# Retention followed by a soft mixture of experts on one core: the transposes to natural layout move in front of the intra-chunk products, the group's logits and dispatch move to a step's end, the selection rounds move later, and the output blocks become 256, 128, 128 columns wide

## The chip, the cores and the metric

The kernel runs on one NeuronCore of a Trainium2 chip. The metric is the device time of one execution in microseconds (us): the median of several runs. One execution was also taken by the hardware profiler; its page and its trace are what is read below. TensorE has two rows in the profile, PE (matmuls) and PEld (weight loads, which overlap them). DVE is VectorE, ACT ScalarE, POOL GpSimd, and SP SyncE, whose queue issues every DMA of this kernel.

## The reference

Four sequences of 768 tokens and 8 heads of width 64 go through a retention (a decaying linear attention), and its output, seen as 3072 tokens of 512 channels, through a soft mixture of 8 experts with 4 slots each:

```
for t: state = gamma[h] * state + k[t] v[t]^T ;  y[t] = q[t] state / 8
x = y as (3072, 512)
logits = x @ phi                                   # 3072 x 32 slots
d = softmax of logits over the tokens  ; slot_in = d.T @ x
slot_out[e] = relu(slot_in[e] @ w1[e]) @ w2[e]     # 512 -> 1024 -> 512, 8 experts
c = softmax of logits over the slots   ; out = c @ slot_out
```

All data are 32-bit floats. The weights w1 and w2 are 33.6 MB of the 55.8 MB read; the output is 6.3 MB.

## The kernel before, in words

**Retention.** There are 24 steps (4 sequences of 6 chunks of 128 tokens). Step i works, on TensorE, in this order: `scores(i+1)` (L225: keys times queries of the next chunk into the two PSUM tiles sc0 and sc1; VectorE masks them, L229, into two tiles A; ScalarE copies the transposed keys, L233, where they are not loaded), `inter(i)` (L247: the state `sst` times the queries into the PSUM tiles y0 and y1), `intra(i)` (L258: v times A, added into y0 and y1), `state(i)` (L280, copied to `sst` by ScalarE, L282; left out in the last chunk of a sequence), and `natural(i-1)` (L288: four transposes of the previous chunk's result into the PSUM bank misc, copied by ScalarE into xn, L290). After `intra(i)`, VectorE's `scale(i)` (L267, two instructions each for y0 and y1) writes the chunk's result yT. There is one buffer of y0, y1, sc0, sc1 and misc each, so `inter(i+1)` waits until `scale(i)` has read y0 and y1. GpSimd multiplies each v by its decay (L207) after its DMA.

**Groups.** Four steps are a group g. In the first step of the next group (ph 0) the logits of the group's 512 tokens are made in misc (`logits_mm`, L300; maximum L320, nm L321, exponential on ScalarE L323, a transposed copy lb on VectorE L328), and at that step's end the exponentials are transposed (`dispatch_p`, L333, copied by ScalarE L335). In the second step (ph 1) `dispatch_u` (L342) multiplies them with the four xn, and VectorE adds that to acc (L353). `combine_weights` makes the softmax over the slots from lb: on VectorE cm (L359), the difference cb (L361), after ScalarE's exponential the sum and its inverse cz (L364 to L366), on GpSimd their product (L367), and on VectorE the transpose into cT (L368).

**Experts.** After step 23 come the last group's logits, `natural(23)`, whose copy to xn is one VectorE instruction, the last dispatch, and the slots' inputs siT. `hidden(g, k)` (L533) multiplies them with w1 for two halves g of the experts; `hidden_t` (L546) transposes the result. `split_c` cuts cT into a rounded part and a rest (VectorE, L384 and L385), and four `c_round(n)` (L395) spread it by a selection matrix into two PSUM buffers named sm, from which ScalarE casts it (L401) into the tiles c4T that the output products need.

**Output.** The 512 output channels are done in blocks. For each, 16 pieces of work fc (L623) multiply with w2; then `finish` copies the sum (L586), spreads it with one matmul (L590), splits it (L592, L593), multiplies it with c4T (L605, six products per 128 channels), copies these out of PSUM on VectorE and ScalarE (L611, L608) and sends 128 channels x 1024 tokens per DMA (L609). `finish` is a generator: its pieces run between the fc of the next block, in places set by the tables Y1, Y2 and BURST; the last block's run alone.

**Queues.** TensorE's order is that of the code. The other engines' orders, and that of the DMAs on SP, are set by the scheduler that builds the program. Weights stream ahead of use: 34 tiles of 512 KB during the retention, then into the key/query buffers (L163), into half tiles (L168) and into freed tiles (L171). kq, v and kn are the DMAs of a step: keys and queries (four buffers), values, and keys in natural layout for some steps.

Of the kernel before, what the change touches and what calls it, by code (L numbers as in the profile page):

```python
# [12 lines left out]
ALU = mybir.AluOpType  # L13
# [3 lines left out]
B, H, S, D = 4, 8, 768, 64  # L17
# [19 lines left out]
NPRE = 34  # L37
BLOCKS = [(0, 128), (128, 256), (384, 128)]
NRING = 34
# [6 lines left out]
FPS = {256: 4, 192: 4, 128: 8, 64: 8}  # L46
Y1 = (3, 4, 2)
Y2 = (4, 6, 2)
GRP = 4
# [42 lines left out]
def retention_soft_moe_kernel(  # L92
# [117 lines left out]
    def scores(i):  # L210
# [5 lines left out]
        for hf in range(2):  # L216
            scv = sct[hf][:, :, 0:384].rearrange("p r (g n) -> p r g n", n=192)
            for gg in range(2):
                g = 2 * hf + gg
                for late in range(2):  # L220
                    for r in range(2):
                        o = (late if g % 2 == 0 else 1 - late) * D
                        kb = KB[2 * g + late]
                        n = 2 + state - late
                        nc.tensor.matmul(scv[o:o + D, r, gg, late * D:(late + n) * D],  # L225
                                         s["kq"][r * D:(r + 1) * D, kb * D:(kb + 1) * D],
                                         blocks(s["kq"], r, NB - (2 - late) * QS[g], QS[g], n),
                                         start=True, stop=True)
            nc.vector.tensor_tensor(A[hf], scv[:, :, :, 0:C],  # L229
                                    mask.unsqueeze(1).broadcast_to([128, 2, 2, C]), ALU.mult)  # L230
            if state:
                kn = s["kn"].rearrange("p (g r) e -> p r g e", r=2)[:, :, 2 * hf:2 * hf + 2]
                nc.scalar.copy(kn, scv[:, :, :, C:C + D])  # L233
# [50 lines left out]
    def natural(i):  # L284
# [4 lines left out]
        s["xn"] = half_tile()  # L289
        (nc.vector.tensor_copy if i == NSTEP - 1 else nc.scalar.copy)(s["xn"], xp)  # L290

# [45 lines left out]
    def dispatch_u(g):  # L337
# [6 lines left out]
        if g == 0:  # L344
            nc.scalar.copy(acc, u)
        elif last:
# [4 lines left out]
        else:  # L351
            nc.vector.scalar_tensor_tensor(zrun, zrun, q["al"], q["z"], ALU.mult, ALU.add)
            nc.vector.scalar_tensor_tensor(acc, acc, q["al"], u, ALU.mult, ALU.add)  # L353

# [72 lines left out]
    scores(0)  # L427
    for e, hs_ in ((nc.gpsimd, slice(4, 8)), (nc.vector, slice(0, 4))):
        e.tensor_tensor(st[0]["v"][:, hs_], st[0]["v"][:, hs_],
                        vsc[:, 0, hs_].unsqueeze(2).broadcast_to([128, 4, D]), ALU.mult)  # L430
    budget = 0.0
    for i in range(NSTEP):
# [6 lines left out]

        def rest():  # L440
            intra(i)
            scale(i)
            state(i)

        if i == 0:
            inter(i)
            rest()
        if not last:
# [7 lines left out]
        if i + 3 < NSTEP:  # L456
            load_kq(i + 3)
        if g > 0 and ph == 0:
            logits_mm(g - 1, range(GRP))
            logits(g - 1)  # L460
        if g > 0 and ph == 1:
            dispatch_u(g - 1)
        if i > 0:
            rest()
        if g > 0 and ph == 1:
            combine_weights(g - 1)
        if i > 0:
            natural(i - 1)
        if g > 0 and ph == 0:
            dispatch_p(g - 1, i)  # L470
    psc_phase.__exit__(None, None, None)
# [96 lines left out]
    hidden_t(0)  # L568
    c_round(0)
    for k in (2, 3):  # L570
        load_weights(4)
        hidden(1, k)
        c_round(k - 1)
    load_weights(len(weights))
    c_round(3)

# [40 lines left out]
    for cb, (c0, w) in enumerate(BLOCKS):  # L617
        op = pe.tile([128, 512], F32, name=("sc0", "sc1")[cb % 2])
        for g in range(2):
            for fc in range(NFC):  # L620
# [6 lines left out]
                if cb == 0 and g == 0 and fc == 2:  # L627
                    hidden_t(1)
                for f in pend:
                    next(f, None)  # L630
# [65 lines left out]
```

## Time and profile before

| | |
|---|---|
| time, median of 3 runs | 176.27 us (175.4 to 176.44) |
| profiled execution | 174.94 us, span 173.0 us |
| TensorE busy | 149.7 us (86%) of the span |
| VectorE, ScalarE, GpSimd busy | 93.2, 48.1, 31.9 us |
| DMA moved | 62.51 MB, mean 361 GB/s |
| mean granted TensorE clock | 0.984 |

The span is the time from the first to the last recorded instruction; the execution's own time is 1.94 us more. The profile's views used here are the page's groups of instructions by line, the chain of work that ended last (each piece follows what released it), the timeline of one engine (with, in brackets, how long the engine had been idle and what ended that), and a table of stretches with each engine's busy time, the granted clock, the share of the DMA engines and what they moved.

### The profile page before, as it was taken

The numbers are of one execution on the slowest core, as the hardware profiler recorded it, in microseconds if no ns is written. First come the engines' busy times: TensorE is split into PE (matmuls) and PEld (weight loads), VectorE is DVE, ScalarE is ACT, GpSimd is POOL, SyncE is SP. The second block draws the span as 40 slices with busy tenths as digits, with TensorE's granted clock in tenths as the row PEclk, the third lists the DMA queues.
The fourth block names the chain that finished last, engine by engine and source line by source line (L and its number), as shares of the span: only waits on it lengthen the run. The fifth ranks groups of instructions, "written<-read, shape, count | busy, mean of one in ns | idle before, by whom it ended". The sixth has DMA issues, their size and how long they took to land.

```text
span 173.0 us, 6469 instructions
## 1 busy us (share of the span) xinstructions
PE 149.7 (86%) x2752; PEld 106.4 (62%) x2752; DVE 93.2 (54%) x278; ACT 48.1 (28%) x122; POOL 31.9 (18%) x46
## 2 busy tenths in 40 slices
PE   8589966999899999979999799999977898999700
PEld 2378955689669767868679668853322493566500
DVE  1566645777876787757775685434132131425720
ACT  2133322343513342324133422310102700303510
POOL 0243214213331322031421322400200000000000
PEclk9999999999999999999999999999999999999985
DMA  5999999999999999999999998999999999444993
GB/s 186 322 408 390 368 403 408 403 392 403 402 397 405 403 401 407 396 405 401 403 403 402 406 405 330 279 352 328 357 412 418 410 405 367 184 194 175 393 405 123
DMA packets 20765, 62.51 MB, mean 361 GB/s; under 512 B 2304, under 2 KB 2688, under 8 KB 20736
## 3 DMA queue, kind: packets, MB, share of 16 engines
q1 hardware_dynamic: 20736, 62.09, 92.9%
q8 instruction: 22, 0.36, 0.9%
q14 instruction: 7, 0.06, 0.1%
HBM read 55.79 MB, written 6.29 MB: 359 GB/s over the span
## 4 chain that ended last, share of the span: by engine, by line
PE 69%; DMA 13%; DVE 6%; issue 5%; SPq 1%; ACT 1%; DVEq 0%
PE y L258 11%; PE sc L225 10%; PE sc L623 9%; PE misc L288 7%; PE y L247 5%; DMA kq<-in_kq_dram 5%; DMA r<-in_w_dram 5%; PE y L533 4%; PE S L280 4%; DMA h<-in_v_dram 3%; PE misc L300 3%; PE misc L342 2%; PE misc L533 2%; PE S L533 2%; PE sm L605 2%
## 5 line engine op out<-in xcount | busy, mean ns | idle before, releaser
L229 DVE TENSOR_TENSOR h<-sc,kt 128x512 f32<-128x512 f32 x48 | 31.4, 686 | 18.6 <-PE sc L225 14.6
L207 POOL TENSOR_TENSOR h<-h,kt 128x512 f32<-128x512 f32 x23 | 24.1, 1049 | 61.8 <-DMA h<-in_v_dram 46.3
L267 DVE SCALAR_TENSOR_TENSOR h<-y,kt,ysc 128x128 f32<-128x128 f32 x96 | 27.3, 343 | 4.5 <-PE y L258 4.2
L258 PE MATMUL y<-h 128*64 128x128 f32 x384 | 26.9, 279 | 3.1 <-DVE h L229 2.1
L225 PE MATMUL sc<-kq 64*64 64x128 f32 (+2 forms) x768 | 26.2, 270 | 2.4 <-issue 0.9
L258 PEld LDWEIGHTS y<-h 128*64 128x64 f32 x384 | 20.8, 136 | 11.2 <-issue 6.8
L225 PEld LDWEIGHTS sc<-kq 64*64 64x64 f32 x768 | 21.3, 133 | 7.1 <-issue 4.0
L288 PE MATMUL misc<-kt,h 128*128 128x128 f32 x96 | 15.6, 285 | 2.4 <-DVE cb L361 1.3
L290 ACT COPY h<-misc 128x512 f32<-128x512 f32 x23 | 13.5, 586 | 14.4 <-PE misc L288 12.5
L282 ACT COPY sst<-S 128x256 f32<-128x256 f32 x20 | 7.4, 372 | 33.6 <-PE S L280 33.5
L280 PE MATMUL S<-h 128*64 128x64 f32 x320 | 13.0, 222 | 1.4 <-issue 1.4
L247 PE MATMUL y<-kq,sst 64*64 64x128 f32 x320 | 13.7, 273 | 0.2 <-issue 0.2
L280 PEld LDWEIGHTS S<-h 128*64 128x64 f32 x320 | 12.2, 138 | 1.5 <-issue 1.5
L288 PEld LDWEIGHTS misc<-kt,h 128*128 128x128 f32 x96 | 10.1, 141 | 4.9 <-issue 2.2
L623 PE MATMUL sc<-r,h 128*32 128x128 f32 (+1 forms) x256 | 12.2, 315 | 0.0
L233 ACT COPY h<-sc 128x256 f32<-128x256 f32 x18 | 6.7, 373 | 15.4 <-DVE h L229 15.4
L247 PEld LDWEIGHTS y<-kq,sst 64*64 64x64 f32 x320 | 10.1, 133 | 0.8 <-issue 0.5
L623 PEld LDWEIGHTS sc<-r,h 128*32 128x32 f32 x256 | 7.8, 109 | 4.3 <-issue 2.3
L533 PE MATMUL y<-r,siT 128*32 128x512 f32 x64 | 8.2, 595 | 0.0
L401 ACT CAST r<-sm 128x256 fp32r<-128x256 f32 x12 | 3.7, 383 | 9.9 <-PE sm L395 9.9
L300 PE MATMUL misc<-h,phis 128*32 128x128 f32 x160 | 5.7, 276 | 0.4 <-issue 0.4
L342 PE MATMUL misc<-h,p 128*32 128x512 f32 x40 | 5.3, 605 | 0.0
(122 smaller groups left out, 145.8 us busy)
## 6 DMA issues: line engine op xcount, KB each, us to landing
r<-in_w_dram SPq DMA_DIRECT2D x54, 512.0 KB, 8.4
kq<-in_kq_dram SPq DMA_DIRECT2D x20, 512.0 KB, 7.8
h<-in_v_dram SPq DMA_DIRECT2D x24, 256.0 KB, 7.6
out_dram<-r SPq DMA_DIRECT2D x12, 512.0 KB, 5.4
h<-in_w_dram SPq DMA_DIRECT2D x12, 256.0 KB, 6.6
h<-in_kn_dram SPq DMA_DIRECT2D x11, 256.0 KB, 7.4
kq<-in_kq_dram SPq DMA_DIRECT2D x4, 544.0 KB, 6.4
kq<-in_w_dram SPq DMA_DIRECT2D x4, 512.0 KB, 7.0
```

The lines of the kernel that those rows point to most:

```text
L207: nc.gpsimd.tensor_tensor(v, v, vsc[:, i % NC, :].unsqueeze(2).broadcast_to([128, H, D]), ALU.mult)
L225: nc.tensor.matmul(scv[o:o + D, r, gg, late * D:(late + n) * D], s["kq"][r * D:(r + 1) * D, kb * D:(kb + 1) * D], blocks(s["kq"], r, NB - ...
L229: nc.vector.tensor_tensor(A[hf], scv[:, :, :, 0:C], mask.unsqueeze(1).broadcast_to([128, 2, 2, C]), ALU.mult)
L247: nc.tensor.matmul(y[b][o:o + D, gl, :], sst[r * D:(r + 1) * D, g, :], blocks(s["kq"], r, NB - 2 * QS[g], QS[g], 2), start=(gl == 0), stop ...
L258: nc.tensor.matmul(y[g // 2][o:o + D, g % 2, :], s["v"][:, 2 * g + r, :], s["A"][g // 2][:, r, g % 2, :], start=(c == 0 and g % 2 == 0), s ...
L267: nc.vector.scalar_tensor_tensor(yT[:, g, :], y[g // 2][:, g % 2, :], ybs[:, c, g:g + 1], ysc[:, g, :], ALU.mult, ALU.mult)
L280: nc.tensor.matmul(S_[r * D:(r + 1) * D, g, :], s["kn"][:, 2 * g + r, :], s["v"][:, 2 * g + r, :], start=(c == 0 and g == 0), stop=True, s ...
L288: nc.tensor.transpose(xp[:, g * 128:(g + 1) * 128], s["yT"][:, g, :], ident)
L290: (nc.vector.tensor_copy if i == NSTEP - 1 else nc.scalar.copy)(s["xn"], xp)
L300: nc.tensor.matmul(q["ltp"][32 * j:32 * j + 32, :], phis[:, p, :], st[GRP * g + j]["yT"][:, p, :], start=(p == 0), stop=(p == NPAIR - 1), ...
L533: nc.tensor.matmul(hp[g][half][32 * j:32 * j + 32, :], siT[:, k, :], w1t[4 * g + j, k][half], start=(k == 0), stop=(k == NK - 1), skip_gro ...
L623: nc.tensor.matmul(op[32 * j:32 * j + 32, :w], hT[fc // 2][:, fc % 2, 4 * g + j, :], t[:, f * w:(f + 1) * w], start=(g == 0 and fc == 0), ...
```

## The change

1. In step i, `natural(i-1)` comes between `inter(i)` and `intra(i)`, where it was the step's end. `logits_mm`/`logits` come at the end of a ph 0 step, `dispatch_p` in the ph 1 step after `intra`, and `dispatch_u` at the end of that step. `combine_weights` is issued after the instruction that updates acc. The multiplication of the first v is issued after the first masks.
2. The last xn copy is cut into 256 columns on ScalarE and 256 on VectorE.
3. `c_round(0)` and `(1)` come after `hidden(1,2)` and `hidden(1,3)`, `c_round(2)` and `(3)` inside the first output block.
4. BLOCKS becomes 256, 128, 128 columns, with other places for the pieces of `finish`. The w2 tensor is laid out to match.

```
-BLOCKS = [(0, 128), (128, 256), (384, 128)]
+BLOCKS = [(0, 256), (256, 128), (384, 128)]
-Y1 = (3, 4, 2)
-Y2 = (4, 6, 2)
+Y1 = (4, 3, 2)
+Y2 = (6, 6, 2)
...
         s["xn"] = half_tile()
-        (nc.vector.tensor_copy if i == NSTEP - 1 else nc.scalar.copy)(s["xn"], xp)
+        if i == NSTEP - 1:
+            nc.scalar.copy(s["xn"][:, 0:256], xp[:, 0:256])
+            nc.vector.tensor_copy(s["xn"][:, 256:512], xp[:, 256:512])
+        else:
+            nc.scalar.copy(s["xn"], xp)
...
-    for e, hs_ in ((nc.gpsimd, slice(4, 8)), (nc.vector, slice(0, 4))):
-        e.tensor_tensor(st[0]["v"][:, hs_], st[0]["v"][:, hs_],
-                        vsc[:, 0, hs_].unsqueeze(2).broadcast_to([128, 4, D]), ALU.mult)
+    with tc.issue_after(st[0]["am"].ins):
+        for e, hv in ((nc.gpsimd, slice(4, 8)), (nc.vector, slice(0, 4))):
+            e.tensor_tensor(st[0]["v"][:, hv], st[0]["v"][:, hv],
+                            vsc[:, 0, hv].unsqueeze(2).broadcast_to([128, 4, D]), ALU.mult)
...
         if i + 3 < NSTEP:
             load_kq(i + 3)
+        if i > 0:
+            natural(i - 1)
+        if i > 0:
+            intra(i)
+            scale(i)
+        if g > 0 and ph == 1:
+            dispatch_p(g - 1, i)
+        if i > 0:
+            state(i)
         if g > 0 and ph == 0:
             logits_mm(g - 1, range(GRP))
             logits(g - 1)
         if g > 0 and ph == 1:
             dispatch_u(g - 1)
-        if i > 0:
-            rest()
-        if g > 0 and ph == 1:
-            combine_weights(g - 1)
-        if i > 0:
-            natural(i - 1)
-        if g > 0 and ph == 0:
-            dispatch_p(g - 1, i)
+            with tc.issue_after(gs[g - 1]["acc"].ins):
+                combine_weights(g - 1)
...
     hidden_t(0)
-    c_round(0)
     for k in (2, 3):
         load_weights(4)
         hidden(1, k)
-        c_round(k - 1)
+        c_round(k - 2)
     load_weights(len(weights))
-    c_round(3)
...
                     hidden_t(1)
+                if cb == 0 and (g, fc) in ((0, 6), (1, 2)):
+                    c_round(2 + g)
```

**The end of the retention.** TensorE in steps 22 and 23, from the last score products to the last `intra`, before (y_1839 and y_1840 are y0 and y1 of step 22, y_1881 and y_1882 those of step 23):

```order
L247 MATMUL y_1839<-kq_86,sst 64x128 x2
L247 MATMUL y_1840<-kq_86,sst 64x128 x2
L258 MATMUL y_1839<-h 64x128 x4
L258 MATMUL y_1840<-h 64x128 x4
L280 MATMUL S<-h 64x64 x8
L288 MATMUL misc<-kt,h 128x128 x4
L247 MATMUL y_1881<-kq_87,sst 64x128 x2
L247 MATMUL y_1882<-kq_87,sst 64x128 x2
L247 MATMUL y_1881<-kq_87,sst 64x128 x2
L247 MATMUL y_1882<-kq_87,sst 64x128 x2
L258 MATMUL y_1881<-h 64x128 x4
```

The same place after the change:

```order
L247 MATMUL y_1839<-kq_86,sst 64x128 x2
L247 MATMUL y_1840<-kq_86,sst 64x128 x2
L288 MATMUL misc<-kt,h 128x128 x4
L258 MATMUL y_1839<-h 64x128 x4
L258 MATMUL y_1840<-h 64x128 x4
L280 MATMUL S<-h 64x64 x8
L247 MATMUL y_1881<-kq_87,sst 64x128 x2
L247 MATMUL y_1882<-kq_87,sst 64x128 x2
L247 MATMUL y_1881<-kq_87,sst 64x128 x2
L247 MATMUL y_1882<-kq_87,sst 64x128 x2
L288 MATMUL misc<-kt,h 128x128 x4
L258 MATMUL y_1881<-h 64x128 x4
```

The transposes (L288) have gone ahead of L258, so that `inter(23)` now stands right behind `state(22)`, with nothing between `intra(22)` and it but those eight state products.

VectorE from the masks of step 22's scores to `scale(22)`, before:

```order
L229 TENSOR_TENSOR h<-sc_88,kt 128x512
L364 TENSOR_REDUCE cz<-cb 128x4
L229 TENSOR_TENSOR h<-sc_89,kt 128x512
L365 TENSOR_SCALAR cz<-cz 128x4
L366 RECIPROCAL cz<-cz 128x4
L368 STREAM_TRANSPOSE cT<-cb 128x128
L353 SCALAR_TENSOR_TENSOR acc<-acc,al,misc 128x512
L267 SCALAR_TENSOR_TENSOR h<-y_1755,kt,ysc 128x128 x2
L267 SCALAR_TENSOR_TENSOR h<-y_1756,kt,ysc 128x128 x2
L229 TENSOR_TENSOR h<-sc_88,kt 128x512
L229 TENSOR_TENSOR h<-sc_89,kt 128x512
L267 SCALAR_TENSOR_TENSOR h<-y_1839,kt,ysc 128x128 x2
```

VectorE from the update of acc of the same group to `scale(22)`, after (lines are four higher here than before):

```order
L357 SCALAR_TENSOR_TENSOR acc<-acc,al,misc 128x512
L363 TENSOR_REDUCE cm<-lb 128x4
L229 TENSOR_TENSOR h<-sc_88,kt 128x512
L365 TENSOR_TENSOR cb<-lb,cm 128x128
L229 TENSOR_TENSOR h<-sc_89,kt 128x512
L368 TENSOR_REDUCE cz<-cb 128x4
L369 TENSOR_SCALAR cz<-cz 128x4
L370 RECIPROCAL cz<-cz 128x4
L372 STREAM_TRANSPOSE cT<-cb 128x128
L267 SCALAR_TENSOR_TENSOR h<-y_1839,kt,ysc 128x128 x2
```

Before, the group's softmax over the slots was through ahead of `scale(21)` (y_1755, y_1756); now all of it, with the transpose cT that needs GpSimd's product, stands between the update of acc and `scale(22)`. On GpSimd, a group's product (L367, now L371) stands behind one more multiplication of a v than before: behind that of v(4g+7), so that the fifth group's comes after v(23)'s.

**Loads.** SP's queue around the keys and queries of step 17 (kq1_85), before, and after:

```order
L194 DMA kq0_84<-in_kq_dram 128x1024
L171 DMA r_1186<-in_w1_dram 128x1024
L171 DMA r_1188<-in_w1_dram 128x1024
L200 DMA h_1223<-in_v_dram 128x512
L204 DMA h_1225<-in_kn_dram 128x512
L194 DMA kq1_85<-in_kq_dram 128x1024
```

```order
L194 DMA kq0_84<-in_kq_dram 128x1024
L171 DMA r_1186<-in_w1_dram 128x1024
L171 DMA r_1188<-in_w1_dram 128x1024
L194 DMA kq1_85<-in_kq_dram 128x1024
L200 DMA h_1223<-in_v_dram 128x512
L204 DMA h_1225<-in_kn_dram 128x512
```

The keys and queries of step 17 have moved ahead of one v and one kn.

**The rounds.** ScalarE from the slots' inputs to the output copies, before (h<-y is the copy of the first half of `hidden(1,3)`, the casts are those of the rounds):

```order
L539 COPY h<-misc 128x512
L401 CAST r<-sm 128x2x128 x8
L539 COPY h<-y_2126 128x512
L401 CAST r<-sm 128x2x128 x4
L608 COPY r<-misc 128x512
```

and after:

```order
L544 COPY h<-misc 128x512
L544 COPY h<-y_2127 128x512
L405 CAST r<-sm 128x2x128 x12
L611 COPY r<-misc 128x512
L611 COPY r<-sm 128x512 x2
```

All twelve casts now stand behind the copy that waits for `hidden(1,3)`.

More of the change, by code (lines that the diff above doesn't have):

```diff
@@ L228, in scores @@
                                          start=True, stop=True)
-            nc.vector.tensor_tensor(A[hf], scv[:, :, :, 0:C],
+            s["am"] = nc.vector.tensor_tensor(A[hf], scv[:, :, :, 0:C],
                                     mask.unsqueeze(1).broadcast_to([128, 2, 2, C]), ALU.mult)
@@ L344, in dispatch_u @@
         if g == 0:
-            nc.scalar.copy(acc, u)
+            q["acc"] = nc.scalar.copy(acc, u)
         elif last:
@@ L352, in dispatch_u @@
             nc.vector.scalar_tensor_tensor(zrun, zrun, q["al"], q["z"], ALU.mult, ALU.add)
-            nc.vector.scalar_tensor_tensor(acc, acc, q["al"], u, ALU.mult, ALU.add)
+            q["acc"] = nc.vector.scalar_tensor_tensor(acc, acc, q["al"], u, ALU.mult, ALU.add)
     def combine_weights(g):
@@ L438, in retention_soft_moe_kernel @@
         budget -= int(budget + 1e-6)
-        def rest():
+        if i == 0:
+            inter(i)
             intra(i)
@@ L443, in rest @@
             state(i)
-        if i == 0:
-            inter(i)
-            rest()
         if not last:
@@ L462, in retention_soft_moe_kernel @@
             dispatch_u(g - 1)
-        if i > 0:
-            rest()
-        if g > 0 and ph == 1:
-            combine_weights(g - 1)
-        if i > 0:
-            natural(i - 1)
-        if g > 0 and ph == 0:
-            dispatch_p(g - 1, i)
+            with tc.issue_after(gs[g - 1]["acc"].ins):
+                combine_weights(g - 1)
     psc_phase.__exit__(None, None, None)
```

## The prediction

> **What bounds the kernel now.** I read the table of stretches first, then the chain of waits, then the timelines of single engines. Columns of the first: us, then busy time (and instructions) of PE, PEld, DVE, ACT and POOL, granted clock, DMA share, GB/s.
>
> ```profile
> 75.60:109.10 33.50, 31.66 (x677) 25.23 (x680) 23.30 (x70) 9.86 (x27) 8.25 (x9) 1.00 1.01 390
> 128.60:137.60 9.00, 6.57 (x49) 2.33 (x48) 3.06 (x16) 3.59 (x11) 0.00 (x0) 1.00 1.03 416
> 137.60:161.50 23.90, 23.09 (x415) 15.15 (x415) 8.89 (x32) 4.76 (x10) 0.00 (x0) 1.00 0.70 277
> ```
>
> Two things run nearly level through the retention: the DMA engines are never idle (share 1.01), and TensorE works 31.7 of 33.5 us. After the retention TensorE leads alone: it idles 2.4 us of the 9 around the selection rounds, and hardly at all in the output blocks, while the DMA engines fall to 0.70. Which of the two leads in the retention is seen where TensorE last waited for data:
>
> ```profile
> 75.59 0.90 PE L225 MATMUL sc<-kq 64*64 64x128 f32 x32 [0.71 <-DMA kq<-in_kq_dram]
> ```
>
> That is the scores of step 17. It is the only wait for keys and queries in the profile; from there to 165 us the chain of waits is TensorE with short hand-overs. So I take 75.6 us as the starting line, and count what TensorE must do and wait for behind it. These are pieces of the chain from there to the last logits (start, us, engine, tile, line):
>
> ```profile
> 77.16 0.35 issue
> 77.51 1.08 PE misc L300 x31
> ...
> 92.75 1.23 PE sc L225 x24
> ...
> 94.43 1.01 PE misc L300 x32
> 95.44 0.95 issue
> ...
> 98.81 0.81 PE sc L225 x24
> ...
> 100.31 0.99 PE misc L342 x8
> ...
> 102.33 0.46 PE S L280 x16
> ...
> 104.26 0.45 PE y L247 x16
> 104.71 1.02 PE y L258 x16
> ...
> 106.20 0.59 PE misc L288 x4
> ...
> 109.10 1.47 PE sm L300 x32
> ```
>
> The reader is to see the price of each piece of a step: scores 0.81 or (with the transposed keys) 1.23, `inter` 0.45, `intra` 1.02, `state` 0.46, `natural` 0.59, logits 1.01, `dispatch_u` 0.99. "issue" is a pause that no engine explains; I assume as many of them after.
>
> **The change, part by part.** Working against the profiled execution (174.94 us, span 173.0); I add the sum to the median of 176.27 at the end.
>
> *Start of step 17: -0.7.* The loads of step 17's keys pass a v and a kn, 0.52 MB, which at 390 GB/s is 1.3 us earlier; the wait of 0.71 goes and TensorE's own arrival (74.9) is late next. Up to there the change takes waits away and adds others of the same sort as below. I count them as equal; the bounds are -0.7 (keys do not arrive before TensorE) and +1 (one more wait as in the fifth group).
>
> *Steps 17 to 20, scores to scores: -0.25.* Before, 92.75 - 75.59 = 17.16, less the pause of 0.35 it is 16.81. The pieces alone sum to 15.0: scores 0.81 + 0.81 + 1.23 + 0.81, `inter` three times (the first chunk of a sequence has none), four `intra` and `natural`, three `state`, logits, dispatch 0.99 and 0.1 for the small transpose. So 1.8 us of small waits go at most. The new ones: 0.5 for lb (worked out below), 0.5 where `dispatch_u` stands at once behind `dispatch_p` with ScalarE's copy between them (step 17 has no `state`), and 0.55 behind VectorE's chain, since `scores(20)` covers most of it. 15.0 + 1.55 = 16.55. Bounds -1.8 and +1.8, the latter if this group loses as much as the next.
>
> *The fifth group and the end of the retention: +1.75.* Before, from the logits to the last logits 109.10 - 94.43 = 14.67, less the pause 13.72. What VectorE and GpSimd need is in the timelines:
>
> ```profile
> 76.24 1.29 DVE L229 TENSOR_TENSOR h<-sc,kt 128x512 f32<-128x512 f32 x2 [1.66 <-PE sc L225]
> ...
> 78.97 0.21 DVE L321 TENSOR_SCALAR nm<-mg,mrun 128x1 f32<-128x1 f32 x1
> ...
> 84.12 0.70 DVE L353 SCALAR_TENSOR_TENSOR acc<-acc,al,misc 128x512 f32<-128x512 f32 x1
> 84.75 1.12 DVE L267 SCALAR_TENSOR_TENSOR h<-y,kt,ysc 128x128 f32<-128x128 f32 x4
> ...
> 118.39 0.28 DVE L364 TENSOR_REDUCE cz<-cb 128x4 f32<-128x128 f32 x1 [0.43 <-ACT cb L362]
> ...
> 118.91 0.18 DVE L366 RECIPROCAL cz<-cz 128x4 f32<-128x4 f32 x1
> 119.24 0.40 POOL L367 TENSOR_TENSOR cb<-cb,cz 128x128 f32<-128x128 f32 x1 [7.17 <-DMA h<-in_w_dram]
> ...
> 119.67 0.31 DVE L368 STREAM_TRANSPOSE cT<-cb 128x128 f32<-128x128 f32 x1 [0.58 <-POOL cb L367]
> ```
>
> First wait: `natural(20)` needs misc, which VectorE's lb must have read. The logits of the fourth group ended at 78.59 (77.51 + 1.08) and nm at 79.18, 0.6 later; behind nm now stand a mask (half of 1.29), a small instruction and lb (0.31 like cT): 0.6 + 0.65 + 0.1 + 0.31 = 1.7 after the logits. TensorE is there after `scores` and `inter`, 1.26, so it waits about 0.5. Second wait: let U be the end of `dispatch_u`. VectorE then does acc (to U + 0.8, with 0.1 for the hand-over), cm 0.28, a mask 0.64, cb 0.28, a mask 0.64, the three cz (118.39 to 119.09: 0.7), waits for GpSimd (0.15 + 0.4), and does cT: U + 4.2. Only then comes `scale(22)`: y0 is free at U + 4.8, y1 at U + 5.35. TensorE, with 0.81 + 0.45 + 0.59 + 1.02 + 0.46, stands at `inter(23)` at U + 3.33 and has nothing to do in between, as there are no more scores. It ends `inter(23)` at U + 5.7 where it would have been U + 3.8: 1.9 lost. Queued behind it are `natural(22)`, `intra(23)` and all that follows.
>
> Summed: 0.59 + 1.02 + 0.46 + 1.01 = 3.08, then step 21 with 0.81 + 0.45 + 0.5 + 0.59 + 1.02 + 0.2 + 0.46 + 0.99 = 5.02, then 5.7 + 0.59 + 1.02 = 7.31; together 15.4 against 13.72, or about +1.75. Bounds: -0.4 if every wait of VectorE is hidden, +3 if GpSimd is late too (a rival below).
>
> *The last copy to xn: -0.1.* Before, one VectorE copy of 0.61 stood on the chain; now ScalarE copies one half, VectorE the other:
>
> ```profile
> 112.18 0.20 ACT wj L498
> ...
> 112.70 0.61 DVE h L290
> ```
> ```profile
> L586 DVE COPY acc<-sc 128x256 f32<-128x256 f32 x1 | 0.4, 424 | 3.2 <-PE sc L623 3.2
> L282 ACT COPY sst<-S 128x256 f32<-128x256 f32 x20 | 7.4, 372 | 33.6 <-PE S L280 33.5
> ```
>
> ScalarE is busy with wj until 112.38, so its half ends at 112.38 + 0.37 = 112.75. In the built program VectorE's half carries a wait for ScalarE's: it ends at 112.8 + 0.42 = 113.2, where the whole copy ended at 113.3. Were the halves side by side, it would be 113.05: a gain of 0.25 at best, and none at worst. [...]
>
> *The rounds: -1.35.* c_round(0) and (1) now stand one place later in the queue, (2) and (3) inside block 0.
>
> ```profile
> 130.05 0.96 DVE L385 TENSOR_TENSOR r<-cT,r 128x768 fp32r<-128x768 f32 x1
> ```
> ```profile
> 131.15 0.49 PE L395 MATMUL sm<-r 32*128 32x512 f32 x2 [0.49 <-DVE r L385]
> ```
> ```profile
> 132.64 0.86 PE S L533 x8
> ```
> ```profile
> 134.20 1.20 ACT L401 CAST r<-sm 128x256 fp32r<-128x256 f32 x4 [1.34 <-PE sm L395]
> 135.36 0.58 ACT L539 COPY h<-y 128x512 f32<-128x512 f32 x1
> ```
>
> Before, block 0 began at 137.60 (third row of the first table). After: hidden_t(0) ends at 128.6 as now; hidden(1,2), two halves of 0.86, to 130.3; the first products of c_round(0) wait for L385 (131.0) and end at 131.6; hidden(1,3) runs to 133.3. Its first half is ready at 132.5, ScalarE copies it from 132.7 to 133.3, and all casts stand behind that copy. At 0.3 each, two casts a buffer, the two sm buffers come free at 133.9 and 134.5, and the last products of c_round(1), 0.75, end at 135.25. So block 0 starts 2.35 earlier; c_round(2) and (3) come back inside it with their products of 0.5, 1.0 in all: -1.35 if their casts hide under block 0's 128 products. Bounds: -1.7 (the products overlap with block 0's hand-overs) and 0, if TensorE waits there for ScalarE as it did ahead of block 0.
>
> *Blocks and tail: +0.54 - 0.95.* Columns are those of the first table; then single instructions (start, us).
>
> ```profile
> 155.00:156.00 1.00, 1.00 (x37) 0.80 (x27) 0.59 (x2) 0.00 (x0) 0.00 (x0) 1.00 0.00 0
> 169.00:170.00 1.00, 0.00 (x0) 0.00 (x0) 0.00 (x0) 0.00 (x0) 0.00 (x0) 0.50 0.91 356
> ```
> ```profile
> 162.84 0.47 PE L605 MATMUL sm<-r,h 128*128 128x512 f32 x1 [0.95 <-DVE h L593]
> ```
> ```profile
> 163.58 0.59 ACT L608 COPY r<-S 128x512 f32<-128x512 f32 x1 [1.21 <-PE S L605]
> ```
> ```profile
> L586 DVE COPY acc<-sc 128x128 f32<-128x128 f32 x2 | 0.6, 286 | 2.2 <-PE sc L623 2.2
> ```
>
> The multiplications are the same in sum. But what stood between block 2's last product and its `rep` product (a copy of 0.286 and two hand-overs) was filled by the last three products of the 256-wide block before it; a 128-wide block before it has none left. A hand-over I take as 0.13, between the 0.03 from POOL to VectorE (119.64 to 119.67) and the 0.27 from TensorE to ScalarE (163.31 to 163.58): +0.54. Against it stands the tail. Before, the DMA engines stood empty at 155 to 156, then nine of twelve outputs came in the last 14 us, and the last byte left at 169.9 (0.91 of the last row), 7.1 behind the last block's first product at 162.84. After, six outputs of the wide first block can leave early and three of the second before the last block ends. Only three remain: first copy done at 163.58 + 0.59 = 164.17, that is 1.33 behind 162.84; from there to the first byte I estimate 0.8 (bounds 0.5 and 1.5; the traces show issue and landing only in sums), and three times 0.52 MB at 410 GB/s is 3.8. Together 6.1 - 7.1 = -0.95. Bounds: 0 if the second block's outputs are still in the queues, -1.5. What follows the last byte (some 3 us in the span) stays.
>
> **The sum.** -0.7 - 0.25 + 1.75 - 0.1 - 1.35 + 0.54 - 0.95 = -1.06. The profiled execution would be 173.9, and from the median of 176.27, 1.3 above the profiled execution, 175.2.
>
> **The rivals.** *Faster: the new waits do not come.* The order of before has waits of its own, over the whole program (busy and mean; idle time and what ended most of it):
>
> ```profile
> L258 PE MATMUL y<-h 128*64 128x128 f32 x384 | 26.9, 279 | 3.1 <-DVE h L229 2.1
> ```
>
> After, the 0.59 of `natural` lies between `inter` and `intra`, so the masks have that much longer, and 2.1 us over 24 steps should go. I set three new waits against it in steps 17 to 20, 1.55 in all. If VectorE has worked off its queue by then, lb is read in time, `dispatch_u`'s copy ends under the `scores`, and `scale` is not late: -1.55 more, -2.6 in sum, 173.7. For it speaks that VectorE is busy 25 of 33.5 us and so has room; against it, that its order is fixed, so that the room may lie elsewhere, as in the fifth group.
>
> *Slower: GpSimd's softmax product waits behind a v.* For each group it stands now behind the multiplication of one more v.
>
> ```profile
> 104.41 1.04 POOL L207 TENSOR_TENSOR h<-h,kt 128x512 f32<-128x512 f32 x1 [2.66 <-PE sc L225]
> ```
>
> This is v(23), ready at 105.45. It decides where the multiplication ends later than U + 3.4, when VectorE would ask for the product: then cT, `scale` and `inter` of the next step but one are late by the difference. For it speaks that the DMA engines are never idle, so that a v lands when the queue comes to it; against it, that in the row above v was not waiting for its DMA, and its reader stood 2 us off. With 0.7 us for each of five groups, two thirds of a multiplication: +3.5, that is 2.5 slower in sum, 178.7.
>
> *It does not do what it says.* If the outputs of block 1 still stand before the last three, and ScalarE makes block 0 wait for the rounds, the -1.35 and the -0.95 shrink to -0.3 together, and a sum of about 0 is left: 176.2.
>
> **How the numbers follow.** Forecast 175.2: chance 0.44, its own range 174.0 to 176.9 (about a third of the summed bounds, since those of seven terms do not all go one way). Faster, 173.7: 0.33, as two of the three new waits are half a microsecond each, no more than the durations they are worked out from can be off. Slower, 178.7: 0.14. Without effect, 176.2: 0.09. One per cent, 1.76 us, is about what a measurement of this kernel can tell from no change. A time under 174.5 is the faster rival and a little of the forecast: 0.34; over 178.0 the slower one: 0.14; between, 0.52. The range 172.7 to 178.2 leaves out half of the slower rival and the far edges of the faster one and of the forecast.
>
> **What would show it.** A wait of `inter(23)` for VectorE's `scale(22)` of 1.4 to 1.9 us, and one of 0.5 of L288 for lb in the second step of a group: the fifth group's term. No wait for keys at `scores(17)`, and these at about 74.9. Block 0 some 2.3 earlier behind hidden_t(0). DMA engines busy between 155 and 158, and the last byte 6.1 behind the last block's first output product. The forecast is wrong if TensorE waits for GpSimd's cb or for a v in several groups (slower), or if no wait over 1 us stands behind `dispatch_u` of the fifth group (faster).

## The result: slower by one per cent

The changed kernel took 179.32 us in the median of 20 runs (176.32 to 183.22), the kernel before 176.36 in 20 runs beside it (174.22 to 177.96, and one of 284.16). The ratio is 1.010, 95% interval 1.006 to 1.015; like every ratio below it compares only runs within 1.5% of their kernel's fastest, 8 of the changed kernel's 20 and not its profiled one, which is why the medians stand 1.7% apart. Forecast were 175.2 and a range of 172.7 to 178.2.

The profiled execution of the changed kernel took 179.28, its span 177.3 (before: 174.94 and 173.0). First the stretches that answer to the three shown of before: scores(17) to the last logits, the rounds, the output blocks. Columns as there.

```profile
78.23:118.17 39.94, 33.64 (x679) 26.39 (x675) 23.22 (x70) 10.80 (x29) 8.05 (x9) 0.96 0.91 325
136.50:144.20 7.70, 6.92 (x56) 2.60 (x53) 3.37 (x19) 1.84 (x6) 0.00 (x0) 1.00 1.03 417
144.20:168.10 23.90, 23.88 (x423) 15.23 (x422) 9.25 (x31) 7.33 (x17) 0.00 (x0) 1.00 0.87 344
```

The retention's stretch lasts 39.9 instead of 33.5 us, its clock is 0.96, and the DMA engines, never idle before, fall to 0.91. The rounds are shorter and the blocks denser. What TensorE waited for, over the whole changed kernel (us in total, times, longest):

```profile
PE misc L288 <- DVE lb L332: 3.2, 5, 0.7
PE y L247 <- issue: 2.0, 2, 1.9
PE y L247 <- DVE h L267: 2.0, 2, 1.5
PE y L337 <- DVE h L267: 1.9, 5, 0.4
...
PE misc L304 <- issue: 1.4, 1, 1.4
...
PE misc L346 <- ACT p L339: 0.7, 2, 0.4
```

The waits for lb and for `scale` come in every group, that for p in two. No wait for keys is left, as forecast, and it is worth nothing: scores(17) starts at 78.23, not at 74.9. The difference of the spans, place by place from the timelines:

| piece | before | after | difference | forecast |
|---|---|---|---|---|
| to scores(17) | 75.59 | 78.23 | +2.64 | -0.7 |
| scores(17) to scores(21) | 17.09 | 21.60 | +4.51 | -0.25 |
| scores(21) to the last logits | 16.35 | 18.34 | +1.99 (+2.9 without before's pause of 0.95) | +1.75 |
| last logits to the slots' first product (L508, now L513) | 5.31 | 5.10 | -0.21 | -0.1 |
| hidden_t(0) to block 0 | 10.01 | 7.65 | -2.36 | -2.35 |
| block 0 to the last block's first output product | 25.24 | 25.67 | +0.43 | +1.54, before had a pause of 0.81 |
| from there to the end | 10.16 | 7.46 | -2.70 | -0.95 |

The end gives 4.8 us, more than forecast; the retention takes 9.1 where 0.8 were expected. In that lies a pause of TensorE in `inter(16)`, right behind scores(17) (the expectations below call the place step 18 and inter(18)), with a stretch at half clock behind it (0.50 from 82.13 to 85.54), which the profile of before does not have ahead of its end (1.00 from 3.55 to 167.39). TensorE's timeline, then the windows (the column before the DMA share is the clock):

```profile
81.42 0.27 PE L247 MATMUL y<-kq,sst 64*64 64x128 f32 x1 [1.85 <-issue]
81.62 0.67 PE L288 MATMUL misc<-kt,h 128*128 128x128 f32 x4
82.22 1.98 PE L258 MATMUL y<-h 128*64 128x128 f32 x16
83.98 1.07 PE L280 MATMUL S<-h 128*64 128x64 f32 x16
```
```profile
82.00:84.00 2.00, 2.00 (x21) 1.82 (x21) 0.61 (x2) 0.58 (x1) 1.04 (x1) 0.53 0.90 334
84.00:86.00 2.00, 2.00 (x46) 1.85 (x48) 0.61 (x3) 0.37 (x1) 0.00 (x0) 0.61 0.89 282
```

`intra`, 1.09 elsewhere, takes 1.98 there, `state` 1.07 instead of 0.63.

### The profile page after: what moved, and what is told of

It reads as the page before. It is cut to its first block, busy times and chain, and to the rows that moved or that the text cites. A ratio compares the mean times of both kernels' runs of the same rounds, so it can differ in the third digit from the quotient of the medians.

```text
span 177.3 us, 6479 instructions
## 1 busy us (share of the span) xinstructions
PE 153.6 (87%) x2752; PEld 107.5 (61%) x2752; DVE 92.5 (52%) x278; ACT 47.8 (27%) x123; POOL 31.7 (18%) x46
## 5 line engine op out<-in xcount | busy, mean ns | idle before, releaser
L258 PE MATMUL y<-h 128*64 128x128 f32 x384 | 27.5, 285 | 1.8 <-DVE h L434 1.6
L258 PEld LDWEIGHTS y<-h 128*64 128x64 f32 x384 | 21.4, 140 | 6.1 <-issue 3.9
L247 PE MATMUL y<-kq,sst 64*64 64x128 f32 x320 | 14.7, 273 | 4.4 <-issue 2.0
L288 PE MATMUL misc<-kt,h 128*128 128x128 f32 x96 | 15.6, 285 | 3.2 <-DVE lb L332 3.2
L288 PEld LDWEIGHTS misc<-kt,h 128*128 128x128 f32 x96 | 10.0, 140 | 9.7 <-issue 4.9
L280 PE MATMUL S<-h 128*64 128x64 f32 x320 | 13.5, 227 | 0.7 <-issue 0.7
L626 PE MATMUL sc<-r,h 128*32 128x128 f32 (+1 forms) x304 | 12.7, 292 | 0.0
L626 PEld LDWEIGHTS sc<-r,h 128*32 128x32 f32 x304 | 8.3, 110 | 4.4 <-issue 2.7
L371 POOL TENSOR_TENSOR cb<-cb,cz 128x128 f32<-128x128 f32 x6 | 2.4, 400 | 27.2 <-DVE cz L370 21.2
L357 DVE SCALAR_TENSOR_TENSOR acc<-acc,al,misc 128x512 f32<-128x512 f32 x4 | 3.0, 747 | 6.3 <-PE misc L346 6.3
```

Source lines behind the costliest of these rows:

```text
L247: nc.tensor.matmul(y[b][o:o + D, gl, :], sst[r * D:(r + 1) * D, g, :], blocks(s["kq"], r, NB - 2 * QS[g], QS[g], 2), start=(gl == 0), stop ...
L258: nc.tensor.matmul(y[g // 2][o:o + D, g % 2, :], s["v"][:, 2 * g + r, :], s["A"][g // 2][:, r, g % 2, :], start=(c == 0 and g % 2 == 0), s ...
L280: nc.tensor.matmul(S_[r * D:(r + 1) * D, g, :], s["kn"][:, 2 * g + r, :], s["v"][:, 2 * g + r, :], start=(c == 0 and g == 0), stop=True, s ...
L288: nc.tensor.transpose(xp[:, g * 128:(g + 1) * 128], s["yT"][:, g, :], ident)
L626: nc.tensor.matmul(op[32 * j:32 * j + 32, :w], hT[fc // 2][:, fc % 2, 4 * g + j, :], t[:, f * w:(f + 1) * w], start=(g == 0 and fc == 0), ...
```

## The experiments

All medians in us; "before" is the kernel before in the same session, and the ratios are taken as above. Differences from the changed kernel are between sessions, so they are given in the medians and in the ratios.

| run | what it is | median | before | ratio, 95% interval |
|---|---|---|---|---|
| e1_order | new order alone | 183.61 | 176.13 | 1.043, 1.034 to 1.052 |
| e2_end | blocks, rounds, last x copy alone | 170.74 | 176.13 | 0.973, 0.968 to 0.978 |
| e3_lb_first | after, lb ahead of the masks | 178.76 | 176.13 | 1.016, 1.008 to 1.023 |
| e4_free5 | after, fifth group's weights not held | 178.22 | 176.13 | 1.003, 0.998 to 1.009 |
| f1_blocks | before, blocks alone | 173.70 | 176.04 | 0.990, 0.985 to 0.994 |
| f2_rounds | before, rounds alone | 172.75 | 176.04 | 0.988, 0.982 to 0.994 |
| f4_nat23 | e2_end, early `natural` in steps 3 and 4 of a group | 171.50 | 176.04 | 0.981, 0.976 to 0.986 |
| f5_best | e2_end, first v products behind the first mask | 170.65 | 176.04 | 0.976, 0.970 to 0.981 |
| g1_free_all | after, no group's weights held | 175.80 | 176.21 | 0.992, 0.987 to 0.998 |
| g2_dp | after, dispatch_p ahead of `intra` | 180.08 | 176.21 | 1.012, 1.006 to 1.019 |
| g3_all | e3, e4 and g2 together | 176.17 | 176.21 | 1.000, 0.996 to 1.005 |
| h1_shift64 | after, 64 instructions ahead | 176.17 | 176.51 | 1.005, 1.001 to 1.009 |
| h2_shift128 | after, 128 instructions ahead | 175.57 | 176.51 | 1.001, 0.997 to 1.004 |
| k1_before128 | before, 128 ahead | 174.97 | 176.28 | 0.991, 0.987 to 0.994 |
| k2_end128 | e2_end, 128 ahead | 171.52 | 176.28 | 0.975, 0.971 to 0.980 |
| k4_free128 | g1_free_all, 128 ahead | 174.53 | 176.28 | 0.997, 0.993 to 1.001 |

**Order or end?** e1_order is the change without

```
-BLOCKS = [(0, 256), (256, 128), (384, 128)]
+BLOCKS = [(0, 128), (128, 256), (384, 128)]
...
+    c_round(0)
...
-            nc.scalar.copy(s["xn"][:, 0:256], xp[:, 0:256])
-            nc.vector.tensor_copy(s["xn"][:, 256:512], xp[:, 256:512])
```

and e2_end is before with just these lines (the last x copy is in it too, which its expectation does not name).

> The new order of the steps alone; blocks, rounds and last x copy as before. Theory O (the order costs what the end gives back): in the profiles the last logits start at 118.17 instead of 109.03, 9.1 later; 3.5 of that is a pause of TensorE of 1.85 and a stretch of 3.4 at half clock that followed it, the rest are waits. So without those this kernel is 5 to 6 slower than before, about 182, and still more where the half clock comes. Rival P (the order is about even, as predicted, and the pause and the half clock are chance): within 1.5 of before, about 177.

> Blocks and rounds of the change alone; the steps in the order of before. Theory O: the end is worth its full pieces in the profile of after, block 0 starts 2.36 earlier after the slots' inputs, the last block's first output product comes 0.4 later behind that, and what follows it is 2.7 shorter: about -4.6, so 171.7. Rival P: the gain of the end is what was predicted, -1.35 + 0.54 - 0.95, so 174.5.

Measured: +7.5 and -5.4 in the medians, +4.3% and -2.7% in the ratios; the two sum to +1.6%, the change has +1.0%. Theory O holds, and P falls on both sides: the order is not even, and the end is worth more than forecast. The half clock has a part in the 7.5: the profile of e1_order has two stretches of it (from 82.6 and from 140.6), and all six runs have a mean clock of 0.969 to 0.979.

**The end, in its parts.**

> The kernel before with the blocks of 256, 128, 128 alone. If the tail's gain belongs to the blocks, it shows whole here: the stretch behind the last block's first output product 2.7 shorter, the products 0.5 later, so about -2.2 from the kernel before (174.0). Rival: the prediction's terms, +0.54 - 0.95, about -0.4; that is what comes out if the last bytes were earlier only because the rounds moved.

> The kernel before with the moved rounds alone. By the profiles block 0 starts 2.8 earlier and takes 0.9 back for two rounds inside it, so -1.9 where the outputs follow; but with the small block first the outputs may still end when the DMA engines have moved them. Theory O: -1 to -2. Rival: 0, the last nine outputs are bound by the DMA engines from 158 on.

The blocks alone give 2.3 (2.2 expected), the rounds alone 3.3 (1.0% and 1.2%); together 5.6, about e2_end's 5.4. The rounds gave more than the -1 to -2 expected: with them alone the outputs begin earlier too (the first output product at 143.8 instead of 146.5). So the expectation's rival, that the DMA engines hold the end anyway, is out.

**Waits of the second step.** In e3_lb_first the masks of that step wait until lb is out:

```
+            if g > 0 and ph == 1:
+                with tc.issue_after(gs[g - 1]["lbi"].ins):
+                    scores(i + 1)
```

> The changed kernel, but on VectorE lb (the transpose that frees the tile misc) stands ahead of both masks in the second step of each group. Theory O: five waits of natural for lb (0.42, 0.71, 0.69, 0.73, 0.69, together 3.2) go, the masks come 0.3 later, which natural covers in part: 2 to 3 faster than the changed kernel, about 175 in undisturbed runs against its 177.5. Rival: the wait only moves to intra, which then waits for the later masks: within 0.7 of the changed kernel.

```profile
PE y L337 <- DVE h L267: 2.1, 5, 0.6
PE y L247 <- DVE h L267: 2.0, 2, 1.6
PE y L247 <- issue: 2.0, 1, 2.0
PE misc L304 <- issue: 1.4, 1, 1.4
...
PE misc L288 <- DVE lb L332: 1.1, 3, 0.4
```

The wait for lb fell from 3.2 to 1.1. The second steps of the five groups last 5.49, 5.83, 5.70, 5.47 and 5.59 here, where the change has 5.49, 5.91, 6.41, 5.79 and 5.89: 1.4 less in all in this profile. In the runs the kernel is not faster (178.76 against 179.32, ratio 1.016 against 1.010). The rival has it for the most part. g2_dp takes the next two waits, for `scale` and p, by moving one call. g2_dp and g3_all leave something out: dispatch_p's transpose is written into a part of the tile y0 that `inter` and `intra` do not use, and where it stands between the two, the second steps' result is incomplete; I take it that `inter`'s part of y0 is missing, which no run shows by itself. The instructions stay the same, so the two serve for their times alone and are no versions to keep.

```
         if i > 0:
             natural(i - 1)
+        if g > 0 and ph == 1:
+            dispatch_p(g - 1, i)
         if i > 0:
             intra(i)
             scale(i)
-        if g > 0 and ph == 1:
-            dispatch_p(g - 1, i)
```

> The changed kernel, but dispatch_p stands ahead of intra instead of behind it in the second step of each group. Theory: its waits for scale (0.36 to 0.42 five times, 1.9 in all) and those of dispatch_u for the copy of p (0.35 twice) go, as the copy lies under intra: 2 to 2.6 faster than the changed kernel in undisturbed runs, about 175. Rival: the second step is bound by VectorE's chain from the logits to the masks and scale, so the wait turns up at intra or at the next step: within 0.7 of the changed kernel.

> The changed kernel with three of its waits taken away at once: lb ahead of the masks, dispatch_p ahead of intra, the fifth group's weights not held behind acc. Theory: the waits for lb, scale and p go together (some 5 in the profile of after) and inter(23)'s 1.5 less 0.5: about 172.5, that is two thirds of the way to e2_end's 170.7. Rival: what stands ahead of the second step's masks on VectorE stays, 174.5 to 175.

g2_dp gives no gain, as its rival says: the second steps went from 5.49, 5.91, 6.41, 5.79 and 5.89 to 5.30, 6.10, 6.08, 5.60 and 5.83, and in four of them `intra` now pauses for 0.8. All three repairs together (176.17) miss both the 172.5 of the theory and the rival's 174.5 to 175. They are 2 under e4_free5 in the median, but only 0.3% in the ratios, where the intervals overlap, and they gain no more than g1_free_all below, which leaves the second steps as they are. I read these waits as one chain on VectorE, from the logits through two masks to `scale`, in which taking one link's wait away shows the next; no run took the whole chain away, so this is not shown.

**The chain behind acc.**

> The changed kernel, but in the fifth group the combine weights are not held behind acc on VectorE, so that cm, cb, cz come ahead of it. Theory O: the wait of 1.54 of inter(23) for scale(22) goes, and dispatch_p waits some 0.5 longer for scale(21): 0.5 to 1.2 faster than the changed kernel. Rival: inter(23) waits as long for scale(22), since acc and the two masks are the longer part of what is ahead of it: no difference.

> The changed kernel, but no group's combine weights are held behind acc. In the changed kernel the third and fourth steps of a group (8 to 9, 12 to 13, 16 to 17) last 1.0, 1.1 and 0.3 longer than before, and inter(23) waits 1.5: the chain acc, cm, mask, cb, mask, cz, cT ahead of scale. Theory: with the chain loosened these go, 3.9 in all, and the second steps give back 0.3 to 0.5 each, since cm and cb now stand ahead of their scale: 1.5 to 2.5 faster than the changed kernel in undisturbed runs, about 175.5. Rival: only the fifth group counts (e4_free5), the others move their wait to the second step: no faster than e4_free5, about 176.

```
-            with tc.issue_after(gs[g - 1]["acc"].ins):
-                combine_weights(g - 1)
+            combine_weights(g - 1)
```

e4_free5 gave what was expected, -1.1 in the median and -0.7% in the ratios, though its interval overlaps the change's; in its profile the wait of 1.54 is one of 0.53. g1_free_all is the largest repair within the order, and more than expected: -3.5 in the median, -1.8% in the ratios. In the change (the chain of waits, near the end of the retention) the links stand one behind the other:

```profile
110.63 0.75 DVE acc L357
111.38 0.20 DVE cm L363
111.58 0.60 DVE h L229
112.17 0.20 DVE cb L365
112.37 0.60 DVE h L229
...
114.08 0.41 POOL cb L371
114.48 0.02 issue
114.51 0.31 DVE cT L372
114.82 0.50 DVE h L267 x2
115.32 0.14 issue
115.45 0.44 PE y L247 x4
```

That is the wait of 1.54 which the prediction foresaw at `inter(23)`. But the same chain stands in the other groups: from scores(8) to scores(9) 4.30 instead of 3.34, from scores(12) to scores(13) 4.03 instead of 2.88. In g1_free_all these two are 3.37 and 2.90 again.

**Is it `natural`?** The steps with nothing but `natural` moved (from scores(7) to scores(8), and those from 11, 15, 19) last 3.32, 3.34, 3.76 and 3.32 in both orders.

> The order of before with the end of the change (blocks, rounds, last x copy: the kernel of e2_end, 170.7), and natural ahead of intra only in the third and fourth step of each group, where no logits or dispatch stand. Theory: steps 7, 11 and 19 lasted 3.32 to 3.34 in both orders, so natural's move alone is worth nothing, and the loss of the new order is that of logits and dispatch: 170.7, within 0.5. Rival: natural's move is a part of the loss, as its copy takes ScalarE ahead of the copies that the states and the scores wait for: 1 or more slower than e2_end.

> The kernel of e2_end, and the first multiplications of v behind the first mask, as in the changed kernel. In the profiles scores(1) came 4.4 after scores(0) instead of 5.2, which the prediction did not count. Theory: TensorE leads until step 16, so -0.7 against e2_end, 170.0. Rival: the keys of a later step come no earlier, since the DMA engines are never idle, and the gain is waited away by step 17: 170.7.

f4_nat23's interval overlaps e2_end's; its 0.8 more in the median is not told from nothing. Not run singly were `natural`'s move in the first two steps of a group and the moves of the logits and of dispatch, so the loss is not divided among these. f5_best equals e2_end: what the first step gains (4.05 instead of 5.20 from scores(0) to scores(1)) is gone by scores(17), which stands at 75.64 (e2_end: 74.38). The rival has the number and not the cause: its profile has no wait for the keys of a later step, but one of 1.1 of `natural` for acc.

**Pauses.** Counted in TensorE's stream of weight loads, multiplications and the semaphore waits among them, the pauses at issue over 0.3 of before and the change stand at the 705th, 961st, 1729th, 3009th, 3777th and 5057th instruction, always 193 past a multiple of 256; other runs have such pauses at the 1985th, 2497th and 3521st too. (The wait of 1.34 that the list of before gives to cb, at 28.1, stands at the 961st too, where the change has a pause of 1.40; it may be the same thing.) The stream has 22 places of that kind, and the trace of the change has 22 transfers on the instruction queue, of 16 KB each:

```profile
q8 instruction: 22, 0.36, 0.8%
```

In all 18 profiles, before and the change included, every pause over 0.2 at these places ends 2.2 to 2.7 after the start of one of these transfers. h1_shift64 and h2_shift128 change only what stands ahead of scores(0):

```
-WARM = 5
-WN = 256
+WARM = 37
+WN = 32
```

> The changed kernel with 21 warm-up products of 64 columns instead of 5 of 256 in about the same time: all of TensorE's later instructions stand 64 further on in its stream (a product is two multiplications and two weight loads). In the profiles TensorE's pauses named issue stand behind its 704th, 960th, 1728th, 3008th, 3776th and 5056th instruction, that is at 192 past a multiple of 256, and the one at the 3008th is 1.85 to 2.0 in the kernels with the new order and 0.35 to 0.95 in those with the old. Theory F (a refill of the instruction buffer at fixed places of the stream): the pause of step 18 moves 64 instructions ahead, from inter(18) into state(17) or intra(17), and may be longer or shorter there; if it falls under 1.2, the half clock behind it goes too, and the kernel is 1 to 3 faster than the changed one (176 to 178 in place of 179). Rival L (the loads of keys and v at that place hold it up): the pause stays at inter(18) with 1.9.

> As h1_shift64, with 37 warm-up products of 32 columns: 128 instructions further on. Theory F: the pause of step 18 moves 128 instructions ahead, into natural(16) or intra(17). Rival L: it stays at inter(18) with 1.9. In time, 176 to 180 by theory F, as the place decides how long the pause is; 179 by rival L.

```profile
PE misc L288 <- DVE lb L332: 2.9, 5, 0.7
PE sc L225 <- DMA kq<-in_kq_dram: 1.9, 1, 1.9
PE y L337 <- DVE h L267: 1.9, 5, 0.4
...
PE y L247 <- DVE h L267: 1.1, 2, 0.7
...
PE y L258 <- issue: 0.8, 2, 0.6
```

In h2_shift128 (above, its waits) the pause behind scores(17) is gone, no stretch at half clock is left in the profile ahead of its end, and the kernel takes 3.7 less than the change in the median, 1.0% in the ratios; h1_shift64, with a pause of 1.33 in scores(18), at the next place of the stream, takes 3.2 less, 0.5% in the ratios. The pauses over 0.3 at these places sum to 3.9 in the change, 2.0 in h1_shift64 and 0.9 in h2_shift128. Rival L is out, and F holds in that the pauses go with the stream; that each would just move 128 instructions ahead was wrong, since most places have none. Of the refill in theory F the traces show the places and the 22 transfers, and no buffer; its limit of 1.2 for the half clock is shown by no run (h1_shift64's pause of 1.33 had none behind it). Of the waits behind VectorE those for lb and `scale` at the second steps stayed (2.9, 1.9); that of `inter` fell from 2.0 to 1.1.

> The kernel before, with the 128 instructions of h2_shift128 ahead of it. In its profile the pauses at the refill places sum to 5.6 (1.38, 1.26, 0.93, 0.35, 0.89, 0.81). Theory F1 (the pauses follow where the places fall, in any order of the steps): they shrink by about as much as in the changed kernel, 2 to 4, and the kernel is 172 to 174. Then the difference between the two orders stays some 3. Rival F2 (the old order's pauses cost nothing more, since the loads of keys hold step 17 anyway): within 1 of 176.

> The kernel of e2_end with the 128 instructions ahead of it. F1: 1 to 3 faster than 170.7. F2: 170 to 171.

> The changed kernel with no group's weights held behind acc (g1_free_all, 175.8, 173.3 where no half clock came), and the 128 instructions ahead of it. If the two repairs add up, 172 to 172.5; what is left against e2_end's 170.7 is then the second steps' waits. If the pauses merely go elsewhere, 174.

The same shift gives before 1.3 and gives e2_end nothing: between F1 and F2, so a shift is no rule, it merely falls well or badly. F1's mechanism did not come: the pauses over 0.3 at these places sum to 5.9 in k1_before128 and 6.6 in k2_end128, where before and e2_end have 5.6 and 5.0. What before gains by it is not explained. At equal shift the new order costs 4.1 (h2_shift128 against k2_end128, 2.5% in the ratios). k4_free128, expected at 172 to 172.5 if the repairs add up and at 174 if not, took 174.5: it has a pause of 1.6 at the 4033rd instruction and a wait of 1.4 of `natural` for acc, neither of which g1_free_all's profile has. The repairs do not add up.

The version that beats both kernels is **e2_end** (with f5_best beside it): 170.7, 2.7% under before.

## Why the prediction was wrong, step by step

- *"Up to there the change takes waits away and adds others of the same sort ... I count them as equal"* is the step that failed first. To scores(17) the change lost 2.64, though the wait for keys went and the first step, which the sum left out, gained 0.8. Nearly every group pays what the prediction worked out for the last one: the second step lasts 1.2 to 1.7 more in four groups and 0.3 in one (lb, `scale`, p), the fourth step of the first two 1.0 and 1.15 more (the chain behind acc), against 0.5 and 0.6 that the first step saves in two.
- *"So 1.8 us of small waits go at most."* The 1.8 were for the most part no waits that could go. The same table of stretches had TensorE idle for 1.84 of 33.5 us, of which 1.5 were pauses; the pieces of 15.0 summed too low, since their prices were read where a piece ran unhindered. One part was a wait counted as busy time, and it went: `intra(17)`, before and after,

```profile
83.39 1.56 PE L258 MATMUL y<-h 128*64 128x128 f32 x16
```
```profile
88.86 1.09 PE L258 MATMUL y<-h 128*64 128x128 f32 x16
```

Little else could go, and the new waits of this stretch, forecast at 1.55, came at 1.50 (lb 0.73, `scale` 0.42, p 0.35); the stretch took about 1.3 more beside pause and half clock, where -0.25 was forecast.
- *"I assume as many of them after"*: the pauses were no more, but one of 0.35 became 1.85 (1.85 to 2.1 in the unshifted kernels with the new order, longer in g2_dp and g3_all; with the old order 0.3 to 1.0, but 1.84 in f1_blocks), and half clock for 3.4 us behind it cost some 1.7 more, by an estimate from its length and its clock of 0.50. No rival had this.
- *Fifth group, +1.75*: right in mechanism (1.54 at `inter(23)`, forecast 1.9; lb 0.69, forecast 0.5), mis-sized: +2.9 without the pause. What was summed as 15.4 took 16.65 (from 101.52 to 118.17): step 21 took 5.90 and not 5.02, with a wait of dispatch_p for `scale` (0.36) that was missing, and `inter(23)` ended at U + 6.0 and not U + 5.7.
- *Last copy, -0.1*: -0.21. ScalarE's half began at 121.42, ahead of wj's end, so its end came before VectorE was free:

```profile
121.22 0.30 ACT L503 ACTIVATE wj<-nmc,nms 128x2 f32<-128x2 f32 x1
121.42 0.36 ACT L291 COPY h<-misc 128x256 f32<-128x256 f32 x1
```
```profile
121.69 0.15 DVE L507 TENSOR_TENSOR zw<-zc,wj 128x2 f32<-128x2 f32 x1
121.81 0.43 DVE L292 COPY h<-misc 128x256 f32<-128x256 f32 x1
```

The halves do stand one behind the other (121.78, 121.81), but VectorE was busy with L507 until then anyway (121.69 and 0.15), so these rows do not show whether the two could have run side by side.
- *Rounds, blocks*: -2.36, as forecast, and block 0 to the last block's first output product +1.24 without before's pause, where 1.54 was forecast; right.
- *Tail, -0.95*: from the last block's first output product to the last packet it took 6.3 (169.84 to 176.12); forecast were 6.1, though the terms there, 1.33 + 0.8 + 3.8, sum to 5.9, and no row shows the 0.8 by itself. What was mis-sized is "what follows the last byte (some 3 us in the span) stays". The windows of before, then of after:

```profile
170.00:171.00 1.00, 0.00 (x0) 0.00 (x0) 0.00 (x0) 0.00 (x0) 0.00 (x0) 0.50 0.06 25
171.00:172.00 1.00, 0.00 (x0) 0.00 (x0) 0.00 (x0) 0.00 (x0) 0.00 (x0) 0.50 0.05 20
172.00:173.00 1.00, 0.00 (x0) 0.00 (x0) 0.00 (x0) 0.00 (x0) 0.00 (x0) 0.50 0.00 0
```
```profile
175.00:176.00 1.00, 0.00 (x0) 0.00 (x0) 0.00 (x0) 0.00 (x0) 0.00 (x0) 0.50 0.93 369
176.00:177.00 1.00, 0.00 (x0) 0.00 (x0) 0.00 (x0) 0.00 (x0) 0.00 (x0) 0.50 0.00 0
```

I read a share of 0.06, 1/16, as one of the sixteen DMA engines: before, it worked two us longer than the rest on its part of the last output, to 171.84; after, the share falls from 0.93 to 0.00 without such a tail. I had taken 169.9 for the last byte; 1.2 follow the last packet in both. So 1.9 of the 2.7 is that one engine, which the forecast did not have, and it may be chance: k1_before128, with the blocks of before, has next to no such tail (8.4 from there to the end, where before has 10.2).
- *The slower rival*, GpSimd's product behind a v, did not decide: TensorE's waits name VectorE, cT waited 0.9 at most for GpSimd, and in the fifth group GpSimd had been idle for 5.3 when the product came.
- *The faster rival* rested on a misreading: its 2.1 "over 24 steps" is one wait, of the first `intra` at 7.89 (1.56 after the change), and VectorE is busy 23.3 of the 33.5 us, not 25. *The rival without effect* does not sum to 0: with -0.3 for the two terms +0.9 is left, or 177.2.

What stays open: why the block of instructions behind the 3009th comes later, against TensorE's arrival there, with the new order. Its transfer started at 78.9 in the change and at 75.0 in before, and TensorE went on 2.5 later in both; TensorE reached the place 0.7 and 2.1 after the start. I did not try what sets that start.

## What to carry to other kernels

Price a reordering in every iteration, and count a residual as waits only if the busy table shows the engine idle for that long, or a piece lasts longer there than elsewhere. A wait that moves from link to link when one link is repaired may be one chain; look for its engine, not for the instruction that waits. Run the parts of a change singly: here a good half and a bad half hid each other, and a shift of 128 instructions was worth 3.7 us in the median (1.0% in the ratios) in one order of the steps and nothing in another.

## What the runs showed of the hardware

In the 18 profiles TensorE's pauses named issue over 0.3 us stand only at the places 256 instructions apart (not at all of them), up to 3.5 us each (g2_dp), and end 2.2 to 2.7 us after a transfer of 16 KB on the instruction queue started (2.46 for the 1.38 of before, 2.58 for the 1.85 of the change); the exceptions are those of 0.4 to 0.8 in the second steps of g2_dp and g3_all. Moving the stream by 64 or 128 instructions moved or removed them in the changed kernel: 3.2 and 3.7 us of 179 in the medians, 0.5% and 1.0% in the ratios. A half clock (0.50) came in the change for 3.41 us (82.13 to 85.54) behind idle time of 1.85, and in e3_lb_first behind a wait of 1.55 at 110; in g2_dp it lasted from 83.6 to 90.4. Behind the pause of 1.97 of e3_lb_first it did not come, nor behind before's 1.38 or one of 2.17 in f1_blocks, so the length of the idle time alone does not tell where it comes. In the change the stretches between changes of the clock last 78.51, 3.41 and 88.75 us, 23, 1 and 26 times 3.413, and in before one of 163.84, 48 times that. What sets them is shown by no run.
